# Zero fills held back for the end, six of eight sa/ca tiles on VectorE, and w_down loads that follow the w_down store

## The chip, the cores and the metric

One core of one Trainium2 chip. The metric is the device time of one execution in microseconds, in runs that are not profiled. The kernel before takes 632.78 us (median of 4; 632.57 to 632.94). Profiled spans are about 2 us shorter than these times.

## The reference, cut

The kernel computes the output and all gradients of one decode step: an adaptive layer norm, attention of 32 heads over the last 4096 of 65536 cached positions, a second adaptive layer norm and a gated feed-forward layer.

```python
sa, ca, ga, sb, cb, gb = (silu(c) @ w_mod).reshape(1, 6, 1, -1) ...   # six modulation vectors
h = layernorm(x) * (1 + ca) + sa
x = x + ga * attention(h, k_cache, v_cache, wq, wo)     # the last W = 4096 positions only
h = layernorm(x) * (1 + cb) + sb
x = x + gb * ((sigmoid(h @ w_gate) * (h @ w_up)) @ w_down)
...
_out, _vjp = jax.vjp(_f, x, k_cache, v_cache, wq, wo, w_gate, w_up, w_down, c, w_mod)
```

The gradients of the two caches are zero at the 61440 unused positions of each of 4 groups. So 126 MB of the outputs are zeros: 120 transfers of 1024 KB from one small tile of zeros, the **fills**. They depend on nothing and can go anywhere. Every weight is read once, and a gradient of its size is written.

## The kernel before

The lists Z_... say how many fills are issued at each place. The feed-forward loop has 14 iterations. In each, the gradient of a w_down block overwrites the block in its buffer (two buffers), as do those of w_up and w_gate (three).

```python
Z_FFN = [3, 0, 3, 1, 4, 0, 3, 1, 4, 0, 3, 0, 3, 0, 4, 2, 3, 2, 3, 1, 3, 6, 0, 3, 1, 7, 3, 1]
...
    def zero(n, after=None):
        for _ in range(n):
            if not zleft:
                return
            ins = nc.gpsimd.dma_start(out=zleft.pop(0).bitcast(FP32), in_=zeros[:, :])
...
    for n in range(NB):
        ...                                    # small vectors, broadcast, matvec
        for jj in range(2):
            outer_dve(wd[:, jj * D:(jj + 1) * D], hh[:, jj:jj + 1], b1k)
        nc.sync.dma_start(out=wd_dram(out_8, n), in_=wd)
        for j in range(KD):
            ttr(ug[:, :, j, :], ug[:, :, j, :], dug_b2, dh2acc[:, n * KD + j:n * KD + j + 1])
            outer_act(ug[:, :, j, :], h2[:, j:j + 1], dug_b2)
            ...
        nc.gpsimd.dma_start(out=dwu_view[:, :, n * FB:(n + 1) * FB], in_=ug[:, 0, :, :])
        st = nc.gpsimd.dma_start(out=dwg_view[:, :, n * FB:(n + 1) * FB], in_=ug[:, 1, :, :])
        if n + 2 < NB:
            dep(load_wd(n + 2), st)            # the w_down load waits for the w_gate store
        zero(Z_FFN[2 * n])
        if n + 3 < NB:
            load_ug(n + 3)
        zero(Z_FFN[2 * n + 1])
...
    for j in range(KD):                        # the end: sa/ca part of the w_mod gradient
        if j % 2 == 0:
            outer_act(s2_t[j], cs_col[:, j:j + 1], dmod_b2)
        else:
            outer_dve(s2_t[j], cs_col[:, j:j + 1], dmod_b2)
        nc.gpsimd.dma_start(out=dwm_view[:, j, 0:2048], in_=s2_t[j])
        zero(0 if j < KD - 1 else len(zleft))
```

Of the kernel before, what the change touches and what calls it, by code (L numbers as in the profile page):

```python
# [20 lines left out]
KD = D // P  # L21
F = 3584
FB = 256
NB = F // FB
# [21 lines left out]
Z_WO = [0, 0, 0, 0, 2, 0, 9, 0]  # L46
Z_LN = 2
Z_UG = [2, 0, 2]
Z_FFN = [3, 0, 3, 1, 4, 0, 3, 1, 4, 0, 3, 0, 3, 0, 4, 2, 3, 2, 3, 1, 3, 6, 0, 3, 1, 7, 3, 1]
Z_T0 = 1  # L50
Z_DWO = [3, 4, 0, 0, 1, 2, 0, 0]
Z_SEC = [1, 1, 3, 0, 1, 1, 4, 1]
# [5 lines left out]
def kernel(  # L58
# [67 lines left out]
                zregions.append(region[:, i * ZW:(i + 1) * ZW])  # L126
    zleft = list(zregions)

    def dep(later, earlier):
        tc.add_manual_dep(later.ins, earlier.ins.name,  # L130
                          mybir.DependencyInfo(mybir.DependencyClass.Sync, mybir.DependencyReason.DATA),
                          reason="pace")


    def zero(n, after=None):
        for _ in range(n):
            if not zleft:
                return
            ins = nc.gpsimd.dma_start(out=zleft.pop(0).bitcast(FP32), in_=zeros[:, :])  # L139
            if after is not None:  # L140
                dep(ins, after)


    def new_ps(name="ps"):
        return psum.tile([P, 512], FP32, name=name, tag="mm")
# [13 lines left out]
    def mulv(out, a, b):  # L159
        return tt(out, a, b, ALU.mult)  # L160
# [4 lines left out]
    def cp(out, a):  # L165
        return nc.vector.tensor_copy(out=out, in_=a)  # L166
# [6 lines left out]
    def ttr(out, w, b, acc):  # L173
        return nc.vector.tensor_tensor_reduce(out=out, in0=w, in1=b, scale=1.0, scalar=0.0,  # L174
                                              op0=ALU.mult, op1=ALU.add, accum_out=acc)
# [28 lines left out]
    def outer_act(out, col, b):  # L204
        return nc.scalar.activation(out=out, in_=b, func=ACT.Copy, scale=col)  # L205

    def outer_dve(out, col, b):
        return ts(out, b, col, ALU.mult)

    def col_to_row_out(col_f, dram_out_row, name):  # L210
        rp = ptp.tile([8, P], FP32, name="rp_" + name, tag="tp")
        nc.tensor.transpose(rp[:, :], col_f, ident_f[:, :])
        rowb = pool.tile([8, P], BF16, name=name + "_orow", tag=name + "_orow")
        cp(rowb, rp[:, :])
        nc.sync.dma_start(out=dram_out_row.rearrange("o (j p) -> (o j) p", p=P), in_=rowb)
# [66 lines left out]
    load_wq(0)  # L282

    zero(Z_INIT)

    tp0 = ptp.tile([P, 24], BF16, name="tp_rows", tag="tp")
# [36 lines left out]
    for j in range(KD):  # L323
        for k in range(KM):
            mm = nc.tensor.matmul(mod_ps[:, k:k + 1], lhsT=wm_t[j][:, k * P:(k + 1) * P],
                                  rhs=cs_bf[:, j:j + 1], start=(j == 0 and k == 0), stop=(j == KD - 1),
                                  skip_group_check=True)
        if j < KD - 1:
            mod_transpose(j)
        zero(Z_MOD[j], mm)  # L330
        if j < 3:
            load_wm(j + 5)
        if j < KD - 1:
            load_wq(j + 1)
# [27 lines left out]
    for j in range(KD):  # L362
        for h in range(HQ):
            mm = nc.tensor.matmul(q_ps[:, h:h + 1], lhsT=wq_t[j][:, h * P:(h + 1) * P],
                                  rhs=h1_bf[:, j:j + 1], start=(j == 0 and h == 0), stop=(j == KD - 1),
                                  skip_group_check=True)
        zero(Z_Q[j], mm)
# [127 lines left out]
    def wd_dram(t, n):  # L495
        return t[n * FB:(n + 1) * FB, :].rearrange("(p j) d -> p (j d)", j=2)

    def load_wd(n):
        return nc.sync.dma_start(out=wd_slot[n % 2], in_=wd_dram(B_w_down, n))

    def load_ug(n):
        nc.gpsimd.dma_start(out=ug_slot[n % 3][:, 0, :, :], in_=wu_view[:, :, n * FB:(n + 1) * FB])  # L502
        nc.gpsimd.dma_start(out=ug_slot[n % 3][:, 1, :, :], in_=wg_view[:, :, n * FB:(n + 1) * FB])
# [65 lines left out]
    def front(n):  # L569
        ug, wd = ug_slot[n % 3], wd_slot[n % 2]  # L570
        r = small[n % 2]
        gu = gu_t[n] = new_acc("gu_ps")
        for col, k in ((2, 0), (0, 1)):
            for jj in range(2):
                for j in range(KD):
                    nc.tensor.matmul(gu[:, col + jj:col + jj + 1], lhsT=ug[:, k, j, jj::2],
                                     rhs=h2_bf[:, j:j + 1], start=(j == 0), stop=(j == KD - 1))
        nc.scalar.activation(out=r["sg"], in_=gu[:, 0:2], func=ACT.Sigmoid)
        nc.scalar.activation(out=r["om"], in_=gu[:, 0:2], func=ACT.Sigmoid, scale=-1.0)

    def front_dve(n):
        wd, r = wd_slot[n % 2], small[n % 2]
        for jj in range(2):
            ttr(junk, wd[:, jj * D:(jj + 1) * D], b1k, r["dhh"][:, jj:jj + 1])
# [3 lines left out]
    for n in range(NB):  # L588
        ug, wd, gu, r = ug_slot[n % 3], wd_slot[n % 2], gu_t[n], small[n % 2]
        dug, hh = r["dug"], r["hh"]  # L590
        mulv(dug[:, 0:2], r["dhh"], r["sg"])
        mulv(dug[:, 2:4], dug[:, 0:2], gu[:, 2:4])
        mulv(dug[:, 2:4], dug[:, 2:4], r["om"])
        cp(r["dug_bf"], dug)
        mulv(hh, r["sg"], gu[:, 2:4])
        cp(r["hh_bf"], hh)
        ps = new_ps("bc_ps")
        ps4 = ps.rearrange("m (k p j) -> m k p j", k=2, j=2)
        for k in range(4):
            nc.tensor.matmul(ps4[:, k // 2, :, k % 2], lhsT=r["dug_bf"][:, k:k + 1].broadcast_to([P, P]),  # L600
                             rhs=ident_bf[:, :], start=(k == 0), stop=(k == 3), skip_group_check=True)
        nc.scalar.copy(out=dug_b, in_=ps[:, :])  # L602
        for jj in range(2):
            for k in range(KD):
                nc.tensor.matmul(ffn_ps[:, k:k + 1], lhsT=wd[:, jj * D + k * P:jj * D + (k + 1) * P],
                                 rhs=r["hh_bf"][:, jj:jj + 1], start=(n == 0 and jj == 0 and k == 0),
                                 stop=(n == NB - 1 and jj == 1), skip_group_check=True)
        for jj in range(2):
            outer_dve(wd[:, jj * D:(jj + 1) * D], hh[:, jj:jj + 1], b1k)
        nc.sync.dma_start(out=wd_dram(out_8, n), in_=wd)  # L610
        for j in range(KD):
            ttr(ug[:, :, j, :], ug[:, :, j, :], dug_b2, dh2acc[:, n * KD + j:n * KD + j + 1])
            outer_act(ug[:, :, j, :], h2[:, j:j + 1], dug_b2)
            if j == 3 and n + 1 < NB:
                front(n + 1)
        if n + 1 < NB:
            front_dve(n + 1)
        nc.gpsimd.dma_start(out=dwu_view[:, :, n * FB:(n + 1) * FB], in_=ug[:, 0, :, :])  # L618
        st = nc.gpsimd.dma_start(out=dwg_view[:, :, n * FB:(n + 1) * FB], in_=ug[:, 1, :, :])
        if n + 2 < NB:  # L620
            dep(load_wd(n + 2), st)
        zero(Z_FFN[2 * n])
        if n + 3 < NB:
            load_ug(n + 3)
        zero(Z_FFN[2 * n + 1])

# [171 lines left out]
    for i in range(KD):  # L798
        j = i
# [18 lines left out]
    addv(dx0, dx0b, dx1)  # L818
    col_to_row_out(dx0, out_1[0], "dx0")

    for j in range(KD):
        if j % 2 == 0:
            outer_act(s2_t[j], cs_col[:, j:j + 1], dmod_b2)
        else:
            outer_dve(s2_t[j], cs_col[:, j:j + 1], dmod_b2)
        nc.gpsimd.dma_start(out=dwm_view[:, j, 0:2048], in_=s2_t[j])
        zero(0 if j < KD - 1 else len(zleft))

    t1 = vt([P, KD], "dc_t1")
    ts(t1, sig_c, -1.0, ALU.mult, 1.0, ALU.add)  # L830
# [40 lines left out]
```

## Time and profile before

| stretch (us from the span's start) | what runs | GB/s |
|---|---|---|
| 20 to 170 | modulation, q, k/v, attention output | 422 |
| 170 to 432 | feed-forward loop | 404 |
| 432 to 590 | wo, wq and k/v gradients | 424 |
| 590 to 610 | last k/v stores | 393 |
| 610 to 616 | the **hole**, in which the queues seem to run dry | 208 |
| 616 to 631.5 | last stores, landing | 371, then 10 |

In the view of stretches each line gives a stretch, its length, the busy time of five engines with counts, the granted TensorE clock, the busy share of the DMA engines and GB/s. The share is a mean over the core's 16 DMA engines.

### The profile page before, as it was taken

The numbers are of one execution on the slowest core, as the hardware profiler recorded it, in microseconds if no ns is written. First come the engines' busy times: TensorE is split into PE (matmuls) and PEld (weight loads), VectorE is DVE, ScalarE is ACT, GpSimd is POOL, SyncE is SP. The second block draws the span as 40 slices with busy tenths as digits, with TensorE's granted clock in tenths as the row PEclk, the third lists the DMA queues.
The fourth block names the chain that finished last, engine by engine and source line by source line (L and its number), as shares of the span: only waits on it lengthen the run. The fifth ranks groups of instructions, "written<-read, shape, count | busy, mean of one in ns | idle before, by whom it ended". The sixth has DMA issues, their size and how long they took to land.

```text
span 631.5 us, 8419 instructions
## 1 busy us (share of the span) xinstructions
PE 183.6 (29%) x3324; PEld 161.7 (26%) x3324; DVE 322.9 (51%) x726; ACT 215.4 (34%) x335; POOL 139.5 (22%) x224
## 2 busy tenths in 40 slices
PE   3977275532031110101111101102420950052440
PEld 3977154522021111101111101101310640042330
DVE  3532055204984552535555334507899760699421
ACT  2741165100044231333333023303686340042561
POOL 1001011113315132333332233222221111122021
PEclk9956598655555555555555555555555755555555
DMA  9999999999999999999999999999999999999986
GB/s 358 422 420 421 420 420 418 425 425 426 420 377 404 400 409 406 400 406 391 395 405 419 400 400 407 421 416 427 415 424 425 423 423 427 420 427 423 398 332 246
DMA packets 42183, 256.42 MB, mean 406 GB/s; under 512 B 4768, under 2 KB 4768, under 8 KB 17568
## 3 DMA queue, kind: packets, MB, share of 16 engines
q0 software_dynamic: 31104, 192.95, 80.4%
q1 hardware_dynamic: 10992, 62.93, 28.6%
q8 instruction: 26, 0.43, 0.3%
q14 instruction: 13, 0.11, 0.0%
q10 hardware_dynamic: 48, 0.01, 0.0%
HBM read 70.26 MB, written 185.60 MB: 405 GB/s over the span
## 4 chain that ended last, share of the span: by engine, by line
DMA 64%; DVE 17%; PE 7%; issue 5%; ACT 3%; POOL 2%; ACTq 0%; SPq 0%; DVEq 0%; POOLq 0%
DMA out_dram<-arena 25%; DMA arena<-in_B_w_down_dram 11%; DVE arena L174 7%; DMA arena<-in_A_wq_dram 7%; DMA arena<-in_A_v_cache_dram 6%; DMA arena<-in_B_w_gate_dram 5%; DMA arena<-in_A_wo_dram 4%; ACT arena L205 3%; DMA out_dram<-zeros 3%; DMA arena<-in_w_mod_dram 2%; DVE junk L174 2%; DVE arena L170 2%; DVE arena L178 1%; DVE fold_ps L178 1%; PE tp_kv L404 1%
## 5 line engine op out<-in xcount | busy, mean ns | idle before, releaser
L139 POOL DMA_DIRECT2D out_dram<-zeros x120 | 65.1, 547 | 209.1 <-DMA out_dram<-zeros 51.3
L174 DVE CUSTOM_DVE_ANT_0 junk<-arena,b1k 128x1024 fp8e4<-128x1024 bf16 x28 | 34.3, 1224 | 111.3 <-DMA arena<-in_B_w_down_dram 110.8
L600 PE MATMUL bc_ps<-ident_bf,dug_bf 128*128 128x128 bf16 x56 | 14.5, 475 | 214.4 <-DVE hh L157 214.4
L205 ACT ACTIVATE arena<-dug_b,h 128x512 bf16<-128x512 bf16 x112 | 71.4, 712 | 15.5 <-DVE dh2acc L174 15.5
L174 DVE CUSTOM_DVE_ANT_0 arena<-arena,dug_b 128x512 bf16<-128x512 bf16 x112 | 69.6, 684 | 0.0
L600 PEld LDWEIGHTS <-dug_bf 128*128 128x128 bf16 x56 | 7.8, 171 | 215.5 <-DVE hh L157 215.5
L602 ACT CAST dug_b<-bc_ps 128x512 bf16<-128x512 f32 x14 | 8.2, 586 | 159.4 <-PE bc_ps L600 159.4
L174 DVE CUSTOM_DVE_ANT_0 arena<-arena 128x1024 bf16<-128x1024 bf16 (+1 forms) x16 | 45.1, 2819 | 28.3 <-DMA arena<-in_w_mod_dram 26.2
L784 PEld LDWEIGHTS <-arena 8*128 8x128 bf16 x256 | 25.8, 131 | 76.7 <-issue 73.1
L174 DVE CUSTOM_DVE_ANT_0 arena<-arena,b1k 128x1024 bf16<-128x1024 bf16 x32 | 37.2, 1218 | 0.0
L502 POOL DMA_DIRECT2D arena<-in_B_w_up_dram x14 | 12.7, 909 | 90.3 <-DMA out_dram<-arena 77.7
L205 ACT ACTIVATE arena<-b1k,o_sh 128x1024 bf16<-128x1024 bf16 x24 | 27.2, 1152 | 11.0 <-DVE do_sh L174 11.0
L788 ACT CAST arena<-ps_kv 128x512 bf16<-128x512 f32 x32 | 16.1, 692 | 41.6 <-DMA out_dram<-arena 41.6
L166 DVE COPY arena<-tp_kv 128x1024 bf16<-128x1024 bf16 x19 | 13.0, 691 | 30.2 <-PE tp_kv L404 20.8
L404 PE MATMUL tp_kv<-ident_bf,arena 128*128 128x128 bf16 x256 | 21.2, 246 | 23.7 <-DMA arena<-in_A_k_cache_dram 13.8
L784 PE MATMUL ps_kv<-DO_hd,arena 8*128 8x128 bf16 x128 | 15.9, 296 | 41.6 <-ACT arena L788 41.6
L790 ACT ACTIVATE arena<-ps_kv 128x512 bf16<-128x512 f32 x32 | 16.1, 625 | 29.0 <-DMA out_dram<-arena 29.0
L313 PEld LDWEIGHTS <-arena 128*128 128x128 bf16 x320 | 25.3, 122 | 0.0
L404 PEld LDWEIGHTS <-arena 128*128 128x128 bf16 x256 | 18.4, 112 | 26.5 <-DMA arena<-in_A_k_cache_dram 14.7
L618 POOL DMA_DIRECT2D out_dram<-arena x14 | 12.6, 902 | 56.1 <-ACT arena L205 51.0
L784 PE MATMUL ps_kv<-Q_hd,arena 8*128 8x128 bf16 x128 | 16.1, 295 | 29.1 <-ACT arena L790 29.1
L407 ACT COPY arena<-tp_kv 128x1024 bf16<-128x1024 bf16 x13 | 13.2, 1012 | 33.0 <-PE tp_kv L404 33.0
(224 smaller groups left out, 481.0 us busy)
## 6 DMA issues: line engine op xcount, KB each, us to landing
out_dram<-zeros POOLq DMA_DIRECT2D x120, 1024.0 KB, 17.9
out_dram<-arena POOLq DMA_DIRECT2D x32, 1024.0 KB, 19.5
out_dram<-arena POOLq DMA_DIRECT2D x36, 512.0 KB, 11.5
arena<-in_A_wq_dram SPq DMA_DIRECT2D x16, 1024.0 KB, 15.3
arena<-in_w_mod_dram SPq DMA_DIRECT2D x8, 1536.0 KB, 19.2
arena<-in_A_wo_dram SPq DMA_DIRECT2D x8, 1024.0 KB, 40.7
arena<-in_B_w_down_dram SPq DMA_DIRECT2D x14, 512.0 KB, 10.9
arena<-in_B_w_up_dram POOLq DMA_DIRECT2D x14, 512.0 KB, 11.2
```

Of the source, the lines that this page charges most:

```text
L139: ins = nc.gpsimd.dma_start(out=zleft.pop(0).bitcast(FP32), in_=zeros[:, :])
L166: return nc.vector.tensor_copy(out=out, in_=a)
L174: return nc.vector.tensor_tensor_reduce(out=out, in0=w, in1=b, scale=1.0, scalar=0.0, op0=ALU.mult, op1=ALU.add, accum_out=acc)
L205: return nc.scalar.activation(out=out, in_=b, func=ACT.Copy, scale=col)
L313: nc.tensor.transpose(tp[:, nb * P:(nb + 1) * P], wm_t[j][:, c0:c0 + P], ident_bf[:, :])
L404: nc.tensor.transpose(tp[:, t8 * P:(t8 + 1) * P], src[:, g, t_ * DH:(t_ + 1) * DH], ident_bf[:, :])
L407: last = nc.scalar.copy(out=o, in_=tp[:, :])
L502: nc.gpsimd.dma_start(out=ug_slot[n % 3][:, 0, :, :], in_=wu_view[:, :, n * FB:(n + 1) * FB])
L600: nc.tensor.matmul(ps4[:, k // 2, :, k % 2], lhsT=r["dug_bf"][:, k:k + 1].broadcast_to([P, P]), rhs=ident_bf[:, :], start=(k == 0), stop=( ...
L784: nc.tensor.matmul(ps[:, t4 * DH:(t4 + 1) * DH], lhsT=rows[32 * g:32 * g + HG, t_ * P:(t_ + 1) * P], rhs=hd[32 * g:32 * g + HG, :], start= ...
L788: nc.scalar.copy(out=o, in_=ps[:, :])
L790: nc.scalar.activation(out=o, in_=ps[:, :], func=ACT.Copy, scale=float(scale))
```

## The change

Its intent: take fills out of the loop, keep ten for the end to close the hole there, and let the w_down load go as soon as the store of its buffer has landed. A sa/ca tile is a block of the gradient of w_mod for the vectors sa and ca; there are eight. VectorE makes one faster than ScalarE, so six go to VectorE instead of four.

```diff
-Z_FFN = [3, 0, 3, 1, 4, 0, 3, 1, 4, 0, 3, 0, 3, 0, 4, 2, 3, 2, 3, 1, 3, 6, 0, 3, 1, 7, 3, 1]
+Z_FFN = [3, 0, 2, 1, 3, 0, 2, 1, 3, 0, 2, 0, 3, 0, 3, 1, 2, 2, 2, 1, 2, 4, 0, 3, 1, 5, 3, 1]
+Z_END = [4, 0, 0, 0, 2, 0, 0, 0, 4]
...
+    keep = [sum(Z_END)]
...
-            if not zleft:
+            if len(zleft) <= keep[0]:
...
         nc.sync.dma_start(out=wd_dram(out_8, n), in_=wd)
+        if n + 2 < NB:
+            load_wd(n + 2)
...
-        if n + 2 < NB:
-            dep(load_wd(n + 2), st)
...
+    keep[0] = 0
+    zero(Z_END[0])
     for j in range(KD):
-        if j % 2 == 0:
+        if j % 4 == 1:
             outer_act(s2_t[j], cs_col[:, j:j + 1], dmod_b2)
...
-        zero(0 if j < KD - 1 else len(zleft))
+        zero(Z_END[1 + j] if j < KD - 1 else len(zleft))
```

## The prediction

> **What bounds the kernel now.** I first read the page's slices, to see which engine is full and where it is not.
>
> ```profile
> DVE  3532055204984552535555334507899760699421
> ACT  2741165100044231333333023303686340042561
> ...
> DMA  9999999999999999999999999999999999999986
> GB/s 358 422 420 421 420 420 418 425 425 426 420 377 404 400 409 406 400 406 391 395 405 419 400 400 407 421 416 427 415 424 425 423 423 427 420 427 423 398 332 246
> ```
>
> Each column is 15.8 us. No compute engine is full for long; the transfers are, in all but the last two columns. So the time is bytes over rate (256.42 MB at a mean of 406 GB/s) plus the places where the queues run dry. Two places fall below the usual 420: columns 12 to 25 (the feed-forward loop, about 400) and the end. The table of stretches puts numbers to them; its last two columns are the busy share of the DMA engines and GB/s.
>
> ```profile
> 20.00:170.00 150.00, 76.41 (x1581) 69.69 (x1579) 58.25 (x112) 43.77 (x49) 19.66 (x35) 0.66 1.10 422
> 170.00:432.00 262.00, 33.90 (x736) 31.99 (x735) 130.23 (x387) 77.50 (x149) 79.77 (x113) 0.50 1.14 404
> 432.00:590.00 158.00, 49.25 (x675) 38.71 (x676) 120.54 (x184) 67.80 (x102) 29.34 (x51) 0.52 1.10 424
> 590.00:610.00 20.00, 12.86 (x157) 10.94 (x155) 2.33 (x12) 11.45 (x24) 3.69 (x7) 0.50 0.96 393
> 610.00:616.00 6.00, 0.66 (x3) 0.28 (x2) 3.11 (x8) 5.97 (x5) 2.57 (x4) 0.50 0.52 208
> 616.00:626.00 10.00, 0.37 (x1) 0.08 (x1) 2.11 (x9) 2.48 (x2) 2.15 (x5) 0.50 0.96 371
> 626.00:631.50 5.50, 0.00 (x0) 0.00 (x0) 0.00 (x0) 0.00 (x0) 0.00 (x0) 0.50 0.03 10
> ```
>
> The loop is slower at a share of 1.14, so it does not lack work; its transfers are slower. The hole is at 610 to 616 us: share 0.52. The timeline of those microseconds tells why.
>
> ```profile
> 607.56 0.53 POOL L792 DMA_DIRECT2D out_dram<-arena  x1 [5.97 <-ACT arena L790]
> ...
> 610.80 7.68 ACT L205 ACTIVATE arena<-arena,cs_col 128x2048 bf16<-128x2048 bf16 x4
> ...
> 611.95 2.06 DVE L170 TENSOR_SCALAR arena<-arena,cs_col 128x2048 bf16<-128x2048 bf16 x3
> ...
> 613.09 1.56 POOL L826 DMA_DIRECT2D out_dram<-arena  x2 [5.00 <-ACT arena L205]
> ...
> 618.77 1.05 POOL L826 DMA_DIRECT2D out_dram<-arena  x2 [0.84 <-DMA out_dram<-arena]
> ```
>
> The last k/v gradient store goes out at 607.56. The next store waits for an outer product that itself waits for the sums behind the last k/v matmuls, so nothing is issued until 613.09, and the queue is empty by 612 (the two microseconds from 612 moved 38 GB/s). All 120 zero fills are gone by 560.9 us.
>
> In the loop, the waits show what w_down costs VectorE, and the queue's own waits what holds its load back.
>
> ```profile
> DVE junk L174 <- DMA arena<-in_B_w_down_dram: 110.8, 12, 20.3
> POOL arena L502 <- DMA out_dram<-arena: 77.7, 10, 9.6
> ...
> SPq L499 <- DMA out_dram<-arena: 220.2, 14, 29.8
> ```
>
> VectorE waits 110.8 us for w_down, in a stage whose DMA is busy all the time: it is waiting for a full queue, not for an idle one.
>
> **What the Trainium skill says.** "DMA: Bandwidth & Descriptors", section Issuing engines are not separate DMA queues: transfers from all issuing engines share the same 16 DMA engines. So moving a load from one moment to another adds no bandwidth; the trace agrees (shares near 1.1 in every full stage). The same page, section Where 436 GB/s comes from, gives 435 GB/s as the fabric's ceiling; here full stages run at 422 to 424.[...] "VectorE: DVE Perf Modes", section The perf-mode tier table, gives 693 ns for a bf16 tensor_scalar of 2048 elements; the trace has 2.06 us for three.
>
> **The change, part by part.** The number of transfers, bytes and arithmetic are the same; only order, engine and one wait change.
>
> *1. Fourteen fills leave the loop.* Its list adds to 64 before and 50 after. A fill is 1024 KB, 1.049 MB. What is one worth there? I fitted the bytes of each kind in 2 us windows from 185 to 430 us of the packet records: the fit gives 427 GB/s for fills, 365 for w_up/w_gate traffic, 398 for w_down. So a fill costs 1.049/0.427 = 2.46 us in the loop, and the loop's end should come 14 x 2.46 = 34 us earlier, if the loop can keep the queues full without them. Does it? Without fills an iteration moves 2.10 MB of w_up/w_gate and 1.05 MB of w_down: 5.75 + 2.63 = 8.4 us. With 50/14 = 3.6 fills it takes 17.2 us of DMA; the leanest iterations (two fills) 13.3 us. VectorE's work in an iteration is 247.49 to 257.97, 10.5 us. So the DMA stays the bound, with little room in the lean iterations.
>
> *2. The w_down load drops its wait for the w_gate store.* Before, a store of w_down issued at 253.18 us and the w_gate store of the same iteration at 260.09; the load went at 271.40, landed 13.5 us later. The w_down store itself lands in 15.1 us median (11.1 at best), so the load could go at about 253.2 + 15.1 = 268.3, or earlier as it no longer shares its queue with a store: 3 to 7 us sooner per iteration. As the DMA is full, this saves nothing by itself: it shortens the loop's chain by about as much as the missing fills shorten the DMA time, and so lets part 1 happen. It can remove the loop's few real dips (294 to 302 us: 371, 352, 354, 338 GB/s, 0.9 us short of 400). I give it 0.5 us net.
>
> *3. Four of the fourteen go later into the k/v and wq stage.* The instruction order shows one more fill at one place and three new ones after it; ten stay for the end. That stage runs at 424 GB/s: four cost 4.2/0.424 = 9.9 us, as they did before. They deepen the backlog there, which may fill part of the dip at 592 to 594 us (295 GB/s; about 0.6 us short).
>
> *4. Ten fills in the end.* Four go right after the last k/v store, two after the fourth sa/ca store, four last. Four are 4.2 MB, 10 us of queue: laid from 608 on (by the old clock) they cover the hole to about 620. The hole: at 410 GB/s the six microseconds should move 2.46 MB and moved 1.25, so 1.21/0.410 = **3.0 us** are won. The ten themselves cost 10.5/0.42 = 25 us there and saved the same in the loop.
>
> *5. Six of eight sa/ca tiles on VectorE.* ScalarE takes 7.68/4 = 1.92 us for a tile, VectorE 0.69. Two serial ScalarE tiles instead of four: the last is done 3.8 us earlier. But with ten microseconds of fills ahead in the same queue this is hidden. Worth 0 beside part 4. (Alone it would have shortened the last stores' wait by some 2 us.)
>
> Sum: -3.0 (hole) - 0.5 (loop's dips) - 0.6 (592 dip) = -4.1; I give back 0.2 for the lean iterations, which makes **632.7 - 3.9 = 628.8 us**.
>
> **Rivals.** *The loop cannot keep up with fewer fills:* the queues would show shares below 1 in the lean iterations, and the 34 us of part 1 would come out as 28 or 30; the total would be 630 to 634. For it: the leanest pair of iterations already dips before, and the POOL queue still waits in order for the w_up store before it reloads. Against: the w_down load goes earlier, which is the longest wait. *The early load brings the loop's rate to 424:* 50 fills and all weights at the clean rate would save up to 91 MB x (1/0.404 - 1/0.424) = 10.6 us and give some 618. For it: the loop is slowest where no fill is in the mix. Against: this is the small rows' own rate (365 GB/s at a share near 1), and no row changes. *The end gets slow:* the last stores run at 387 GB/s and if fills did too, ten would cost 1.9 us more than in the loop: 630.5. Against: those are 4 KB packets; fills with 8 KB rows made 426 GB/s before. *Hidden anyway:* everything but the hole is bytes over rate, which is the main line of the sum.
>
> **Range and chances.** The hole's 3.0 us is the firm part; the loop can go 4 us either way. So 628.8, with 625 to 632. Faster by over 2% needs below 620, which only the second rival gives: 0.04. Slower by over 2% (645) needs a loop that loses a third of the moved time: 0.01. Within 2%: 0.95.
>
> **What would show it.** The stretch between the last k/v store and the first sa/ca store should run above 380 GB/s with no two microseconds under 200. The loop should end 32 to 36 us earlier (before: about 432) at 398 to 408 GB/s. VectorE's wait for w_down should fall by over half from 110.8 us, while the wait of the POOL queue for stores stays or grows. The sa/ca tiles should be done well before their stores are issued, which then wait for earlier transfers. I am wrong if the loop shows shares below 1 for more than some 8 us, or its rate rises above 412, or a new hole opens between 540 and 600 us.

## The result, and the profile after

The changed kernel takes 631.33 us (median of 4; 631.13 to 631.72), the kernel before 632.78. The ratio is 0.9978 (95% interval 0.9961 to 0.9995). The gain is 1.4 us where 3.9 were predicted.

The page's slices of the changed kernel (40 columns, here of 15.7 us), to be held against the two rows of before:

```profile
DMA  9999999999999999999999999999999999999994
GB/s 350 425 419 421 420 421 419 425 423 427 421 380 397 402 400 406 405 402 407 410 401 406 385 411 411 420 421 424 423 424 426 425 419 428 427 427 423 422 427 160
```

The hole is gone: full columns to the last but one. By the prediction's own measure everything came true there, and yet the time hardly moved. The stretches of the changed kernel show where it went:

```profile
382.00:580.00 198.00, 58.04 (x773) 45.64 (x774) 118.19 (x176) 73.67 (x116) 37.61 (x68) 0.53 1.11 424
580.00:590.00 10.00, 3.60 (x63) 3.22 (x60) 5.24 (x16) 6.16 (x7) 5.46 (x8) 0.50 1.06 417
590.00:619.00 29.00, 0.37 (x1) 0.08 (x1) 1.71 (x9) 0.00 (x0) 6.40 (x12) 0.50 1.11 424
619.00:626.00 7.00, 0.00 (x0) 0.00 (x0) 0.00 (x0) 0.00 (x0) 0.00 (x0) 0.50 0.14 50
626.00:629.50 3.50, 0.00 (x0) 0.00 (x0) 0.00 (x0) 0.00 (x0) 0.00 (x0) 0.50 0.00 0
```

Almost all bytes are down at 619 to 620 us; then something trickles for 6 us. In steps of two microseconds:

```profile
616.00:618.00 2.00, 0.00 (x0) 0.00 (x0) 0.00 (x0) 0.00 (x0) 0.00 (x0) 0.50 1.14 426
618.00:620.00 2.00, 0.00 (x0) 0.00 (x0) 0.00 (x0) 0.00 (x0) 0.00 (x0) 0.50 0.76 279
620.00:622.00 2.00, 0.00 (x0) 0.00 (x0) 0.00 (x0) 0.00 (x0) 0.00 (x0) 0.50 0.11 37
622.00:624.00 2.00, 0.00 (x0) 0.00 (x0) 0.00 (x0) 0.00 (x0) 0.00 (x0) 0.50 0.07 25
624.00:626.00 2.00, 0.00 (x0) 0.00 (x0) 0.00 (x0) 0.00 (x0) 0.00 (x0) 0.50 0.06 20
```

A share of 0.06 is one engine of 16, and 25 GB/s is a sixteenth of 424, nearly. **One DMA engine ends 5 us after the fifteen others, and the kernel waits for it** (I call it the late engine, or the laggard). The same trickle stands in the middle of the kernel before, where I had read an idle queue:

```profile
608.00:610.00 2.00, 2.00 (x27) 2.00 (x24) 0.48 (x5) 1.29 (x3) 0.09 (x1) 0.50 0.95 385
610.00:612.00 2.00, 0.66 (x3) 0.28 (x2) 1.11 (x6) 1.97 (x3) 0.00 (x0) 0.50 0.77 311
612.00:614.00 2.00, 0.00 (x0) 0.00 (x0) 2.00 (x4) 2.00 (x2) 0.91 (x1) 0.50 0.09 38
614.00:616.00 2.00, 0.00 (x0) 0.00 (x0) 0.00 (x1) 2.00 (x2) 1.66 (x4) 0.50 0.70 275
```

The share of 0.09 at 612 us is the late engine at work, with a little from a second one. The trace has a finer record: every transfer issued from GpSimd gives 16 completion marks. That each belongs to one engine is borne out below, where relieving 1, 9 or 8 engines brings as many marks forward. The **lag** is the time from the 15th mark to the 16th. Times are from the first instruction.

| | last transfer, median mark | 15th mark | last mark | lag |
|---|---|---|---|---|
| kernel before | 625.9 | 626.6 | 628.5 | 1.9 |
| changed kernel | 619.8 | 620.8 | 626.0 | 5.2 |

The lag grows in both, though not steadily. In the kernel before it is 0.4 us at 200 us, 1.3 at 300, 2.6 at 400, about 6 at 580, and 6.1 just ahead of the hole; right after the hole it is 3.3. In between it swings, to 11.5 at 513 us and back to 5.6 at 563, about the time when SyncE's loads of wq and w_mod are in the queues too; why was not tested. The hole itself shows it best: of the last k/v store ahead of it, the median mark comes at 612.0, the 15th at 613.5 and the last at 618.6, when the others are already at the next stores. In the changed kernel the lag is 0.5 to 1.7 around 300, 2.0 at 400, 4.6 at 580 (after a swing to 9.1 at 476) and 5.3 from 599 on.

So the fifteen gained 6 us from the change, and the one that counts gained 2.5. Of these 2.5 the span gained 1.9: from the last mark to the end of the span pass 2.9 us before and 3.6 after. All 18 traces agree in this: 2.9 us in the nine kernels whose last transfers are sa/ca stores, 3.5 to 3.8 in the nine that issue fills last. So **fills in the last place go with some 0.6 us more behind the last landing.** Why is not shown, and no run changed that alone.

The loop. Its two longest waits on transfers, before 110.8 and 77.7 us, are now:

```profile
POOL arena L505 <- DMA out_dram<-arena: 93.3, 10, 11.6
...
DVE junk L177 <- DMA arena<-in_B_w_down_dram: 14.6, 7, 4.7
```

The columns are the total in us, the number of waits and the longest. VectorE hardly waits for w_down any more. GpSimd's wait for the w_up store, before it may load into that buffer, is now the longest wait on a transfer. The sum that opens the gradient stage (line L219 before, L222 after) comes at 437.5 us before and at 383.2 after.

### The profile page after: what moved, and what is told of

Read it like the earlier page. It is cut to its first block, busy times and chain, and to the rows that moved or that the text cites. A ratio compares the mean times of both kernels' runs of the same rounds, so it can differ in the third digit from the quotient of the medians.

```text
span 629.5 us, 8417 instructions
## 1 busy us (share of the span) xinstructions
PE 185.2 (29%) x3324; PEld 162.1 (26%) x3324; DVE 325.8 (52%) x728; ACT 212.8 (34%) x333; POOL 141.0 (22%) x224
## 4 chain that ended last, share of the span: by engine, by line
DMA 66%; DVE 13%; PE 6%; ACT 5%; issue 4%; POOL 3%; ACTq 0%; POOLq 0%; SPq 0%; DVEq 0%
DMA out_dram<-arena 35%; DMA arena<-in_B_w_gate_dram 8%; DMA arena<-in_A_wq_dram 7%; DVE arena L177 7%; DMA arena<-in_A_v_cache_dram 6%; DMA out_dram<-zeros 4%; DMA arena<-in_A_wo_dram 4%; ACT arena L791 1%; ACT arena L208 1%; DVE arena L181 1%; DVE fold_ps L181 1%; POOL out_dram L623 1%; PE tp_kv L407 1%; DMA rows<-in_c_dram 1%; POOL arena L506 1%
## 5 line engine op out<-in xcount | busy, mean ns | idle before, releaser
L579 PE MATMUL gu_ps<-h_bf,arena 128*128 128x1 bf16 x448 | 16.0, 166 | 129.9 <-issue 97.8
L579 PEld LDWEIGHTS <-arena 128*128 128x128 bf16 x448 | 14.1, 105 | 131.9 <-issue 98.3
L177 DVE CUSTOM_DVE_ANT_0 junk<-arena,b1k 128x1024 fp8e4<-128x1024 bf16 x28 | 34.2, 1223 | 15.1 <-DMA arena<-in_B_w_down_dram 14.6
L581 ACT ACTIVATE sg<-gu_ps 128x2 f32<-128x2 f32 x14 | 2.4, 171 | 94.8 <-PE gu_ps L579 94.8
L407 PEld LDWEIGHTS <-arena 128*128 128x128 bf16 x256 | 19.0, 114 | 26.1 <-DMA arena<-in_A_k_cache_dram 14.6
L316 PEld LDWEIGHTS <-arena 128*128 128x128 bf16 x320 | 24.5, 119 | 0.0
## 6 DMA issues: line engine op xcount, KB each, us to landing
arena<-in_A_wq_dram SPq DMA_DIRECT2D x16, 1024.0 KB, 14.6
arena<-in_B_w_down_dram SPq DMA_DIRECT2D x14, 512.0 KB, 10.5
```

The lines of the kernel that those rows point to most:

```text
L177: return nc.vector.tensor_tensor_reduce(out=out, in0=w, in1=b, scale=1.0, scalar=0.0, op0=ALU.mult, op1=ALU.add, accum_out=acc)
L316: nc.tensor.transpose(tp[:, nb * P:(nb + 1) * P], wm_t[j][:, c0:c0 + P], ident_bf[:, :])
L407: nc.tensor.transpose(tp[:, t8 * P:(t8 + 1) * P], src[:, g, t_ * DH:(t_ + 1) * DH], ident_bf[:, :])
L579: nc.tensor.matmul(gu[:, col + jj:col + jj + 1], lhsT=ug[:, k, j, jj::2], rhs=h2_bf[:, j:j + 1], start=(j == 0), stop=(j == KD - 1))
```

## The experiments

**The state of the experiments.** The throw-away output of the w_down reduction is in bf16. Room comes from letting four small row tiles share one buffer and putting one short-lived tile into a free corner of the big one:

```diff
-    junk = vt([P, D], "junk", FP8)
+    junk = vt([P, D], "junk", BF16)
-        rowb = pool.tile([8, P], BF16, name=name + "_orow", tag=name + "_orow")
+        rowb = pool.tile([8, P], BF16, name=name + "_orow", tag="orow")
-    rows24 = vt([24, P], "rows24", BF16)
+    rows24 = pool.tile([24, P], BF16, name="rows24", tag="orow")
-    prod2 = vt([P, 2 * HQ], "prod2")
+    prod2 = ar(F_OFF + 17.5, 0.25).bitcast(FP32)
```

Theories: the **mean-rate theory** of the prediction (time is bytes over the mean rate plus the microseconds in which the queues are empty) and the **laggard theory** (time is what the one late engine needs; what the others gain while it works is worth nothing). The medians below are to be held against the kernel before in the same rounds, 632.97 to 633.14 us.

### Controls

The kernel before with the edit above:

> Control. The check before the chip takes no experiment with the throw-away output of the w_down reduction in fp8, so every experiment writes it in bf16 and frees the room by letting three small row tiles share one buffer. This is the kernel before with only that. Both theories: 632.8 us within 0.6; if it is off by more, all experiments are to be read against it and not against the kernel before.

The changed kernel with it:

> Control: the changed kernel with the bf16 throw-away tile alone. Both theories: 631.3 us within 0.6.

Measured: 632.94 us (ratio 1.0000, interval 0.9986 to 1.0013) and 631.61 (0.9978, 0.9966 to 0.9991). The edit makes no difference beyond the noise.

### Sparing one engine, and loading others

First I tried to relieve the late engine. By the Trainium skill ("DMA: Bandwidth & Descriptors", Why a DMA increments its semaphore by 16 and not by 1) a SyncE transfer of n rows runs on the lowest-numbered k of the 16 engines, k being the largest number up to 16 that divides n. 120 rows leave out engine 15. The expectations take 27 GB/s for one engine, a sixteenth of the 426 GB/s above.

```diff
+    def spare(n):
+        for _ in range(n):
+            r = zleft.pop(0)
+            zf = zeros.bitcast(FP32).rearrange("p (o x) -> p o x", o=1)
+            for lo, hi in ((0, 120), (120, 128)):
+                nc.sync.dma_start(out=r[lo:hi, :].bitcast(FP32).rearrange("p (o x) -> p o x", o=4),
+                                  in_=zf[0:hi - lo, :, :].broadcast_to([hi - lo, 4, 512]))
...
-    zero(Z_END[0])
+    spare(2)
+    zero(Z_END[0] - 2)
```

> The changed kernel, with two of the four fills that follow the last k/v store issued from SyncE in two pieces, 120 rows and 8 rows, so that by the skill's rule for how many engines a transfer uses the highest-numbered of the 16 DMA engines carries nothing of them (64 KB less each, 131 KB in all, 4.8 us at 27 GB/s). Laggard theory (one DMA engine ends 5.2 us after the 15 others and sets the end; the hole in the kernel before was time in which it caught up): 627 us, 4 to 5 us under the changed kernel, if the laggard is that engine; 631.5 if it is another. Mean-rate theory (the missing gain was lost in the loop or in the rate of the end, all engines alike): 631.3 to 631.8, no gain. So a gain of over 3 us proves the laggard; no gain leaves it open.

Measured: 632.78 us (ratio 0.9995, 0.9983 to 1.0008), 1.2 us *slower* than the changed kernel in the same rounds. The marks say why: one engine now ends at 617.2, over 3 us ahead of the next at 620.5, and the last at 627.4. The spared engine exists and isn't the late one; the late one got the extra work. Left open by this alone: no gain was also what the mean-rate theory said.

Next, the opposite: one fill with rows in counts of 119, 7 and 2, which by that rule load engines 0 to 6 alone.

```diff
-            for lo, hi in ((0, 120), (120, 128)):
+            for lo, hi in ((0, 119), (119, 126), (126, 128)):
...
-    spare(2)
-    zero(Z_END[0] - 2)
+    low7(1)
+    zero(Z_END[0] - 1)
```

> The changed kernel, with one of the four fills after the last k/v store issued from SyncE in pieces whose row counts (119, 7 and 2) put it, by the skill's rule, on DMA engines 0 to 6 alone: those get some 86 KB more than in the changed kernel (3.2 us), engines 7 to 15 get 64 KB less (2.4 us). The run that spared engine 15 showed that this one isn't the laggard. Laggard theory: if the laggard is one of 7 to 14, 1.5 to 2.4 us faster than the changed kernel, 629.2 to 630.1; if it is one of 0 to 6, 3 us slower, about 634.7. Mean-rate theory (all engines alike): the seven loaded engines become the last, about 3 us slower, 634 or more.

Measured: 634.91 us (1.0028, 1.0013 to 1.0043), 3.4 us above the changed kernel. Nine marks of the last transfer come at 619.2 to 619.3, six at 623.0 to 623.9, one at 629.5. Nine engines spared, seven loaded, and the late one is among the seven: it moved by 3.5 us, from 626.0. The time followed it. Had the seven been alike, the end would have been at 624, ahead of the changed kernel's.

The same with sixteen pieces of 8 rows, on engines 0 to 7:

```diff
-            for lo, hi in ((0, 119), (119, 126), (126, 128)):
-                nc.sync.dma_start(out=r[lo:hi, :]...
+            for i in range(16):
+                nc.sync.dma_start(out=r[8 * i:8 * i + 8, :]...   # source zf[0:8]
```

> The same with that fill on engines 0 to 7 (sixteen pieces of 8 rows): engine 7 gets 64 KB more instead of 64 KB less. Laggard theory: if engine 7 is the laggard, as the skill's table names it beside 15 as usually slower, 2 to 3 us slower than the changed kernel, 633.5 to 634.5; if the laggard is one of 8 to 14, as fast as the run on engines 0 to 6. Mean-rate theory: about 2.4 us slower, and no difference to the run on 0 to 6 but that of 22 KB.

Measured: 637.11 us (1.0062, 1.0047 to 1.0077). Eight marks come at 619.8 to 620.0, seven between 622.8 and 626.7, the last at 632.2. The rule for k holds again. But this run does not single out engine 7, as I had meant it to: the run before shows the late engine among 0 to 6. The engines got fewer bytes here (128 KB each from this fill, against some 150), and still the delay grew from 3.5 to 6.2 us. So here sixteen small transfers cost the late engine more than three larger ones with more bytes; my expectation had left that out.

To find which of the seven, a fill in pieces of 2 to 7 rows, so that engine 0 gets the most and engine 6 the least:

```diff
+        for n in (2, 3, 4, 5, 6, 7) * 2 + (64, 10):
+            nc.sync.dma_start(out=r[lo:lo + n, :]..., in_=zf[0:n, :, :]...)
+            lo += n
```

> Which engine is the laggard? The changed kernel, with one of the last fills cut into pieces of 2 to 7 rows (twice) on SyncE, then 64 and 10 rows. By the skill's rule DMA engines 0 and 1 get 72 KB more than in the changed kernel, engine 2 56 KB, 3 40 KB, 4 24 KB, 5 8 KB, 6 8 KB less. At 27 GB/s the last landing should move from 626.0 us by +2.7 us if the laggard is engine 0 or 1, +2.1 for 2, +1.5 for 3, +0.9 for 4, +0.3 for 5, -0.3 for 6. Mean-rate theory: no engine is special, under 0.5 us.

One look: 632.46 us (a single run, state unknown). The last mark is at 627.1, 0.9 us after the control's 626.2, which is what engine 4 should give. I don't take it for settled: other marks are spread to 625.3, further than bytes explain, so the pieces' own cost blurs the grades.

The attempt to relieve engines 0 to 6 with odd row counts from GpSimd, two fills:

```diff
+            for m in (7, 81, 7, 27):
+                nc.gpsimd.dma_start(out=r[lo:lo + m, :].bitcast(FP32), in_=zeros[0:m, :])
+                lo += m                        # the last 6 rows from SyncE
```

> The changed kernel, with two of the last fills issued from GpSimd in pieces of 7, 81, 7 and 27 rows (6 rows left go from SyncE). If, as the skill says for GpSimd's transfers, such counts take 7 and 9 engines in turn, engines 0 to 6 carry 80 KB less in all and 7 to 15 64 KB more: laggard theory 2 to 3 us faster than the changed kernel, 628.6 to 629.6. If they are instead spread over 14 engines from the first on, the laggard gets 48 KB more and it is about 2 us slower. Mean-rate theory: 631.5 or slower, the 7 to 15 being last.

Measured: 633.63 us (1.0010, 0.9995 to 1.0025). The last mark moved from 626.2 to 627.7. Nothing was relieved. The second branch of the expectation fits, but the marks of engines that would have been spared don't show it, so where these pieces went stays open. This run is inconclusive.

### The parts of the change alone

The six tiles on VectorE alone, in the kernel before:

```diff
-        if j % 2 == 0:
+        if j % 4 == 1:
             outer_act(s2_t[j], cs_col[:, j:j + 1], dmod_b2)
```

> The kernel before with six sa/ca tiles on VectorE and nothing else: the last stores are issued up to 2 us earlier, the hole at 612 us gets narrower. Mean-rate theory: about 1.5 us faster, 631.3. Laggard theory: the engine that sets the end was busy through the hole anyway, so at most 0.4 us, 632.4 to 632.9.

Measured: 633.10 us (1.0002, 0.9990 to 1.0015). Last mark 628.2, lag 1.2. No gain, as the laggard theory has it.

The early w_down load alone:

```diff
         nc.sync.dma_start(out=wd_dram(out_8, n), in_=wd)
+        if n + 2 < NB:
+            load_wd(n + 2)
...
-        if n + 2 < NB:
-            dep(load_wd(n + 2), st)
```

> The kernel before with only the early w_down load; 64 fills in the loop, hole at the end as before. Prediction on record: worth 0.5 us, as the DMA is full in the loop: 632.4. Laggard theory: worth what it changes of the laggard's lag at the end of the loop, which fell from about 3.0 to 1.4 us with the whole change: 631.3 to 632.9. The rival that the loop's chain was the bound would give 628 or less.

Measured: 630.89 us (0.9964, 0.9948 to 0.9981), and in the repeat below 630.92 against 633.02. **This part alone is worth 2.1 to 2.3 us, more than the whole change.**

The fills alone (both lists and the places of the change; load and tiles as before):

> The kernel before with only the fills moved (50 in the loop, ten held for the end), w_down load late and tiles 4 to 4. Laggard theory: the hole is filled and gives at most 0.5 us, and the loop with fewer fills but the late load can lose some time to a chain that is now longer than its transfers: 632 to 635. Mean-rate theory (prediction on record): the hole's 3 us are won, 629.5 to 630, if the loop keeps up without the early load.

Measured: 634.83 us (1.0026, 1.0012 to 1.0041), slower than the kernel before, by more than the expectation of the prediction could allow. The loop tells it. From 200 to 300 us, first this run, then the early load alone:

```profile
200.00:300.00 100.00, 13.75 (x312) 13.26 (x312) 55.64 (x168) 34.09 (x66) 32.11 (x43) 0.50 1.07 387
```

```profile
200.00:300.00 100.00, 14.41 (x280) 13.23 (x280) 58.03 (x171) 32.10 (x60) 32.90 (x46) 0.50 1.15 408
```

The kernel before ran these 100 us at 402 GB/s and the changed kernel at 405. With fewer fills and the late load the loop's chain is too long for its transfers. In steps of 2 us the queues do run dry: from 288 to 290 us the share is 0.32, at 121 GB/s. VectorE had stood 11.2 us for a w_down load until 275.8, was then busy until 286.6, and the next stores went out at 288.3. Part of the 1.7 us is not the loop's: the last mark comes 0.9 us later than before the change (629.4 against 628.5), the rest passes behind it, as fills come last. With the early load the loop keeps up, but below what the early load can do with all 64 fills.

The changed kernel without its tiles, and the early load with the tiles:

```diff
-        if j % 4 == 1:                # fills and early load, tiles 4 to 4
+        if j % 2 == 0:
```

> The changed kernel with the sa/ca tiles again four to four: tells what the six tiles on VectorE are worth behind the held-back fills. Both theories: 0, as fills cover the queue then; within 0.5 us of the changed kernel, 631.0 to 632.0.

```diff
-        if j % 2 == 0:                # early load, no fill moved, tiles 6 to 2
+        if j % 4 == 1:
```

> The kernel before with the early w_down load and the tiles six to two, and no fill moved, in the same rounds as the changed kernel's relatives: laggard theory: as the early load alone, 630.6 to 631.2, so 0.5 us or so faster than with the fills moved. Mean-rate theory: the hole's 3 us are missing, 2 to 3 us slower than with the fills moved.

Measured in the same rounds: 631.33 us (0.9976, 0.9960 to 0.9993) and 630.96 (0.9965, 0.9950 to 0.9980). The tiles are worth nothing in either company, and with the early load the kernel with its hole open is not slower than the one with the hole filled.

### The hole by itself

Still, in all these runs the hole was closed together with fills taken from the loop. The last group leaves the loop alone. The control is the early load alone again.

> Control of this group: the kernel before with the early w_down load alone, again. Both theories: 630.9 us within 0.5, the hole as it was.

Closing the hole with four fills that stood at the loop's very end, behind its last load:

```diff
-Z_FFN = [ ... 3, 6, 0, 3, 1, 7, 3, 1]
+Z_FFN = [ ... 3, 6, 0, 3, 1, 3, 3, 1]
+    keep = [4]
-            if not zleft:
+            if len(zleft) <= keep[0]:
...
+    keep[0] = 0
+    zero(4)
     for j in range(KD):
```

> The early w_down load, and four of the seven fills at the very end of the loop (its last but one iteration, after its last load) held back for the place right after the last k/v store. All other fills and the stage between stay. Mean-rate theory: the hole's 3 us are won, 627.9 to 628.5. Laggard theory: 15 engines end 3 us earlier, the last one where it did: 630.4 to 631.2, with a lag of over 5 us at the last landing instead of 1.9.

Widening it by idle ScalarE tiles ahead of the first (one, then two):

```diff
+    for _ in range(1):                # 2 in the second run
+        outer_act(s2_t[0], cs_col[:, 0:1], dmod_b2)
     for j in range(KD):
```

> The early w_down load, and one idle ScalarE tile more ahead of the first sa/ca store, so that the hole gets 1.9 us wider and nothing else changes. Mean-rate theory: 1.9 us slower than the control, 632.8. Laggard theory: the lagging engine has work for all of it (its lag was 6.5 us before the hole, the hole was 3.5): 0 to 0.4 us slower, 630.9 to 631.3.

> The same with two idle tiles, 3.8 us. Mean-rate theory: 3.8 us slower, 634.7. Laggard theory: the lag is used up near the end of the hole: 0.5 to 1.5 us slower, 631.4 to 632.4, and all 16 engines end within 1 us of each other.

Measured, all in the same rounds:

| | median us | ratio (95% interval) | median mark | 15th mark | last mark | lag |
|---|---|---|---|---|---|---|
| hole closed | 630.44 | 0.9959 (0.9946 to 0.9971) | 619.3 | 620.6 | 625.6 | 5.0 |
| control | 630.92 | 0.9966 (0.9954 to 0.9979) | 623.5 | 624.2 | 626.2 | 1.9 |
| 1.9 us wider | 630.89 | 0.9967 (0.9954 to 0.9979) | 625.2 | 625.9 | 626.3 | 0.4 |
| 3.8 us wider | 632.50 | 0.9991 (0.9977 to 1.0005) | 627.1 | 627.3 | 627.8 | 0.5 |

The control, then the run with one idle tile:

```profile
610.00:612.00 2.00, 0.00 (x0) 0.00 (x0) 1.63 (x3) 2.00 (x2) 1.28 (x2) 0.50 0.09 38
612.00:614.00 2.00, 0.00 (x0) 0.00 (x0) 0.31 (x1) 2.00 (x2) 1.33 (x3) 0.50 0.83 324
614.00:624.00 10.00, 0.38 (x1) 0.08 (x1) 1.79 (x9) 2.10 (x2) 2.11 (x4) 0.50 0.93 361
```

```profile
610.00:612.00 2.00, 0.00 (x0) 0.00 (x0) 1.79 (x3) 1.97 (x2) 0.00 (x0) 0.50 0.08 34
612.00:614.00 2.00, 0.00 (x0) 0.00 (x0) 0.17 (x1) 2.00 (x2) 1.06 (x2) 0.50 0.07 29
614.00:624.00 10.00, 0.38 (x1) 0.08 (x1) 1.87 (x9) 4.30 (x3) 3.17 (x6) 0.50 1.00 389
```

The run with the hole closed:

```profile
606.00:612.00 6.00, 0.00 (x0) 0.00 (x0) 0.28 (x1) 0.00 (x0) 1.60 (x3) 0.50 1.08 416
612.00:618.00 6.00, 0.00 (x0) 0.00 (x0) 0.00 (x0) 0.00 (x0) 1.07 (x2) 0.50 1.03 417
620.00:626.00 6.00, 0.00 (x0) 0.00 (x0) 0.00 (x0) 0.00 (x0) 0.00 (x0) 0.50 0.06 23
```

With one idle tile fifteen engines are idle for some two microseconds more and the time is the same to 0.03 us. With 3.8 us more it rises by 1.6 us: the late engine has caught up and idles too. Closing the hole brings the fifteen to their end 4 us earlier (median mark 623.5 to 619.3) and the time gains 0.5 us. The runs of the two don't overlap (630.27 to 630.59 against 630.84 to 630.98), though the intervals do. This settles it for the laggard. The run with the hole closed is also the fastest kernel: 630.44 us, against 632.78 and 631.33.

## Why the prediction was right or wrong

**What bounds the kernel: half right.** It is bound by transfers, and no compute engine ever was the limit. But "bytes over rate" was taken over the mean of 16 engines. At the end the bound is one engine. This is the step that carried the error.

**Part 4, the hole, is the step that failed.** "1.21/0.410 = 3.0 us are won" took the mean share of 0.52 for missing work. The engine that sets the end had work all through the hole. Measured: 0.5 us for closing it, 0.0 for widening it by 1.9.

**Part 2, the early load, was mis-sized:** 0.5 us predicted, 2.1 measured. The reasoning "the DMA is full, so this saves nothing by itself" overlooked that the loop's rate depended on it: with this part alone, 402 GB/s became 408 over 200 to 300 us. The wait of VectorE fell as foreseen and further than "by over half", from 110.8 to 14.6 us in the changed kernel.

**Part 1, fourteen fills out of the loop,** was entered as neutral (34 us saved there and spent later). It costs. Alone, with the hole filled, it made the kernel 1.7 us slower (634.83 against 633.14), and the loop's end came 28.0 us earlier (409.5 against 437.5) and not 34. That is the figure of the rival "the loop cannot keep up", which stood at 0.2 in my sum. The step that failed is "so the DMA stays the bound": it held an iteration's transfers against VectorE's 10.5 us of work and left out VectorE's wait for the load. The rival's sign, a share below 1, is there in steps of 2 us (0.32), though the mean of 100 us is 1.07. With the early load, the changed kernel is about 1 us slower than the kernel with only the hole closed (631.61 or 631.33 against 630.44, across rounds). Of this, 0.4 to 0.6 us come before the last mark (626.0 and 626.2 against 625.6), and 0.6 behind it, where fills come last. No part of the prediction had priced that end. How the first half divides between the loop and the four fills moved to a later stage was not measured.

**The sum, re-made:** early load -2.1, hole -0.5, the other moved fills about +0.5 before the last mark and +0.6 behind it, tiles 0: -1.5, measured -1.4. The predicted sum was -3.0 - 0.5 - 0.6 + 0.2. That the time still fell between 625 and 632 is luck: a part priced at 0.5 brought 2.1, and covered most of what the hole did not bring. (In the rival of the slow end, the ten fills at 387 GB/s cost 10.5/0.387 - 25 = 2.1 us more and not 1.9.)

**Part 5, the tiles, was right:** 0 in each of three settings. The remark that alone they would shorten the last stores' wait "by some 2 us" was about the wait and not the time; the time did not change.

**Part 3** put 0.6 us on the dip at 592 us. The dip is gone (424 GB/s from 590 us on), but the lag was 5.2 us at 593 us, so that like the hole it was a dip of the others. What it was worth by itself was not measured.

**The small rows.** The rival that the early load lifts the loop's rate was set aside as "this is the small rows' own rate". (The rows of w_up and w_gate are 512 B, by the kernel.) The records don't bear that out: from 200 to 300 us before the change, the median packet of these transfers takes 174 ns for 4 KB and that of the fills 348 ns for 8 KB, the same per byte. And the early load did lift the rate, if only by 6 GB/s.

**The signs to look for.** The loop's end came 54 us earlier (383.2 against 437.5), where I had given 32 to 36: with the early load alone it came at 407.6, and transfers queue up behind it. The rate of the stretch lay in my band (402 against 398 to 408). The hole did close. The waits went as foreseen, and none of the signs of being wrong appeared. No sign that I named looked at single DMA engines; none could have shown a late one, which is why, but for the loop's end, they came true and the time did not.

## What to carry to other kernels

When a kernel is bound by DMA, read the last microseconds first: a mean share near 1/16 there says that one engine is still at work. In this kernel the gaps of the others then cost nothing until it had caught up. A dip in the mean rate is only worth filling if the last engine is idle in it; a test that widens the dip by a known time is cheap and tells. A load that waits for more than its own buffer is worth freeing even where the queues look full (2.1 us here). Before fills are taken out of a loop, count an iteration's chain with its waits and not only with its work. And look at what is issued last: here fills in that place went with 0.6 us more behind the last landing.

## What the Trainium skill lacked or had wrong

- "DMA: Bandwidth & Descriptors", Latency and other measured facts, names DMA engines 7 and 15 as usually slower. Here engine 15 (by the same page's rule for k) was not the late one: spared, it ended at 617.2 us and the late one at 627.4. The late engine is one of 0 to 6 (nine spared marks at 619.2, the late one at 629.5); which one, and why it lags, stays open.
- No page says that such a lag adds up over a kernel. Here it grew, with swings, from 0.4 us at 200 us to 6.1 at 611, and it stood still at 5.2 to 5.4 from 599 us to the end of the changed kernel.
- No page says what the kind of the last transfers costs behind the last landing. Here it was 2.9 us with sa/ca stores last and 3.5 to 3.8 with fills last.
- "Perfetto Trace Analysis", What "DMA-bound" means, lists specific DMA engines as a bound and is right. It lacks how to see one in a mean: here a share of 0.06 to 0.11 for the last 6 us.
- The rule for k ("DMA: Bandwidth & Descriptors", Why a DMA increments its semaphore by 16 and not by 1) held for transfers from SyncE: 119 rows left nine engines free, 8 rows eight. For GpSimd's transfers of 7, 81 and 27 rows no run here confirms it.
- On small transfers, Rules for kernel authors on the same page say that below 64 KB one pays mostly overhead. The page gives no cost per engine for a transfer cut into such pieces: here sixteen transfers of 64 KB on eight engines held the late engine up by 6.2 us, three larger ones with more bytes for it by 3.5.
